# Second visit of a two-pass mixing: a switch from plain products to the seven-product scheme after block 5

## The chip, the cores and the metric

The kernel runs on one core of one Trainium2 chip. The metric is the device time of one execution in microseconds, as the median over the runs shown. Beside it there is one execution recorded by the hardware profiler. Names of engines: PE is TensorE (PEld its weight loads), DVE is VectorE, ACT is ScalarE, POOL is GpSimd and SP is SyncE.

## What is computed

The input is a batch of 8 sequences of 5696 positions with 128 channels. A long convolution by FFT comes first, and a mixing over positions follows. The reference, cut to what matters:

```python
# y: output of the convolution, (8, 5696, 128)
theta = y @ w_theta
zr, zi = y * cos(theta), y * sin(theta)
u = y + einsum('ts,bsd->btd', w_tok_r, zr) + einsum('ts,bsd->btd', w_tok_i, zi)
out = u + maximum(u @ w_ch, 0)
```

The change lies in the two einsums. Each is a 5696 x 5696 matrix, read in float32 and used in bfloat16, times a 5696 x 1024 operand.

## The kernel before

**Tiles and passes.** The 5632 positions that make up 44 whole tiles of 128 are cut into two halves of 22 tiles; a remainder of 64 is handled apart. The inner dimension is cut in two passes (p = 0 and 1), and in each pass it is cut into 11 blocks (j = 0 to 10). One *visit* (p, tt) makes four output banks of 128 x 512: two output tiles, tt and 22 + tt, for two halves of the batch. Pass 0 makes the visits tt = 0, 1, 2 and so on; "visit 1" below is its second one, tt = 1. Each visit walks through the 11 blocks in four *stretches* of 3, 3, 3 and 2 blocks. The program numbers the stretches through: visit 0 has stretches 0 to 3, visit 1 has 4 to 7, and visit 2 has 8 to 11.

**Two ways of doing one block.** The work of a visit is a 2 x 2 matrix of weights (w11, w12, w21, w22) times a 2 x 2 matrix of operands (b11, b12, b21, b22). A *plain* block takes 8 products of two matmuls each, 16 matmuls in all, straight into the four output banks. The *seven-product* scheme, in the order M3, M4, M5, M2, M1, M7, M6 (`ORDER`), takes 7 products of two matmuls each, so 14 per block. For these it needs sums of weights (`w_sum`, line 924, five for each stretch: M5, M2, M1, M7, M6) and sums of operands (`sum_ops`, line 852, five for each block, kept for all later visits of the pass). It accumulates in seven banks. At the end of the visit, 12 additions on DVE (line 1349) put the seven banks together into the four outputs. A plain visit of pass 0 instead adds its addend on PE (lines 1307 and 1310) and copies the four banks out on ACT (line 1312). `plain(p, tt)` (line 641) says that visits 0 and 1 of pass 0, and visit 0 of pass 1, are plain.

**Weights.** POOL issues the loads (line 690) into a ring of six slots (`ring`, `pump`); a slot comes free when the last stretch that reads it has been transposed. Four loads make a chunk: blocks 0 to 5 or blocks 6 to 10 of one visit. DVE transposes each stretch's four weights (`w_t`, line 915). `prepare(i)` writes these transposes and, for the seven-product scheme, the weight sums of stretch i. It is called at the head of stretch i - 1, so the program has them one stretch ahead. In the last stretch of a visit its steps are woven between the products instead.

**Buffers for the weight sums.** Transposed weights live in a pool of five buffers. Weight sums live in another, `sumpool`, with four (line 871), and a plain stretch also puts its w21 and w22 there.

**The operand sums of pass 0.** `owed` lists the five sums of each block. The first three write new tiles. The last two overwrite b12 and b21, which plain products still read. `sum_some(n)` (line 860) writes up to n of those that are allowed: sums 0 to 2 at any time, and sums 3 and 4 once `done["used"]` has passed the block. A plain stretch calls it up to nine times (six in the last one), and a seven-product stretch seven times.

**Order of the work.** From visit 0 to the middle of visit 2 (the end of stretch 9), `tc.manual_schedule(engines={DVE})` holds DVE to the order in which the program writes its instructions. Outside of it, and for the other engines, a planner orders instructions by the program's order and its own estimate of when they are ready.

**Background work.** `aside` puts a piece of other work into each stretch but the last of a visit. Its first half is four transposes on PE (line 943) and a copy on ACT (line 945). Its second half, `phases_b`, is four matmuls (line 574), then ACT, then DVE (line 578), then ACT (lines 598, 599, 602), then DVE (lines 612 and 613), then stores. It uses the tiles `red` and `mag`, or in the second stretch of a visit the buffers `c2` and `c3`.

Of the kernel before, what the change touches and what calls it, by code (L numbers as in the profile page):

```python
# [22 lines left out]
def kernel(  # L23
# [44 lines left out]
    NJ = QR // 64  # L68
    CJ = 6
    TJ = 3  # L70
# [564 lines left out]
    CHUNKS = [(j0, min(CJ, NJ - j0)) for j0 in range(0, NJ, CJ)]  # L635
# [2 lines left out]
    ring = {"n": 0, "read": set(), "wl": 0, "upto": 0}  # L638
    loaded = {}

    def plain(p, tt):

        return tt == 0 or (p == 0 and tt == 1)

    def loads_of(k):

        p, tt, c = chunks[k]
        loaded[k] = {}

        def one(n, a, row0, ng):  # L650
            loaded[k][n] = load_w(a, row0, p, *CHUNKS[c], ng=ng)
        if tt is None:
            return [lambda n=n, a=a: one(n, a, 2 * H, 2) for n, a in enumerate((moe_w_tok_r, moe_w_tok_i))]
        src = [(a, h * H + tt * P, 4) for h in range(2) for a in (moe_w_tok_r, moe_w_tok_i)]
        return [lambda n=n: one(n, *src[n]) for n in ((0, 1, 2, 3) if plain(p, tt) else (0, 3, 1, 2))]

    queue = [(k, f) for k in range(len(chunks)) for f in loads_of(k)]
    first_of = {}
# [160 lines left out]
    bts_of = {0: {}, 1: {}}  # L819
# [30 lines left out]
    def sum_ops(bt):  # L850
        b11, b12, b21, b22 = (bt[q] for q in (M2, M6, M7, M5))
        return [lambda f=f, x=x: f(*x) for f, x in (  # L852
            (nc.vector.tensor_sub, (bt[M3], b12, b22)), (nc.vector.tensor_sub, (bt[M4], b21, b11)),
            (nc.vector.tensor_add, (bt[M1], b11, b22)), (nc.vector.tensor_add, (b12, b11, b12)),
            (nc.vector.tensor_add, (b21, b21, b22)))]

    done = {"used": 0}
    owed = []

    def sum_some(n):  # L860

        for o in [o for o in owed if o[1] <= 2 or done["used"] > o[0]][:n]:
            owed.remove(o)
            o[2]()

# [25 lines left out]
        spread.extend(bg_phase(t, h) for t in list(range(24, 34)) + [22, 23, 44] + list(range(34, 44)) for h in range(2))  # L891
        spread.extend(bg_left(g) for g in range(0, NT, 4))

    for j in [*range(1, 6), 0, *range(6, NJ - 2), NJ - 1, NJ - 2]:
        owed += [(j, k, lambda j=j, k=k: sum_ops(bts_of[0][j])[k]()) for k in range(5)]

    def next_steps(n):
        for _ in range(min(n, len(steps1))):
# [114 lines left out]
    tags, where_bg = {"n": 0}, {}  # L1013
# [69 lines left out]
    for k, (p, tt, c) in enumerate(chunks):  # L1083
        j0, nj = CHUNKS[c]
        for s0 in range(0, nj, TJ):
            stretches.append((k, p, tt, j0, s0, min(TJ, nj - s0)))
    def prepare(i, at_once=True):
        if i >= len(stretches):
            return None
        k, p, tt, j0, s0, nj = stretches[i]  # L1090
        pump()

        def read():
            if s0 + nj == CHUNKS[chunks[k][2]][1]:
                ring["read"].add(k)
                pump()
        if tt is None:
            a1, a2 = (w_t(loaded[k][n], s0, nj, ng=2) for n in range(2))
            read()
            return a1, a2, w_sum(a1, a2, add, nj, m=64)  # L1100
        w11, w12, w21, w22 = (loaded[k][n] for n in range(4))
        if plain(p, tt):
            a = {}

            def some(n):
                if n in (0, 1):
                    a[n] = w_t((w11, w12)[n], s0, nj)
                elif n in (4, 5):
                    a[n - 2] = w_t((w21, w22)[n - 4], s0, nj, pool=sp)
            if not at_once and p:  # L1110
                return a, some
            for n in range(6):
                some(n)
                if p and n in (1, 4):
                    late_sums(8 if n == 1 else 4)
            read()
            return a if at_once else (a, lambda n: None)
        a = {}

        def step(n):  # L1120

            if n == 0:
                a[M3] = w_t(w11, s0, nj)
            elif n == 1:
                a[M4] = w_t(w22, s0, nj)
            elif n == 2:
                a["12"] = w_t(w12, s0, nj)
                a[M5] = w_sum(a[M3], a["12"], add, nj)
            elif n == 3:
                a["21"] = w_t(w21, s0, nj)  # L1130
                a[M2] = w_sum(a["21"], a[M4], add, nj)
            elif n == 4:
                a[M1] = w_sum(a[M3], a[M4], add, nj)
            elif n == 5:
                a[M7] = w_sum(a["12"], a[M4], ALU.subtract, nj)
            else:
                a[M6] = w_sum(a["21"], a[M3], ALU.subtract, nj)
        if at_once:
            for n in range(7):
                step(n)  # L1140
            read()
            return a
        return a, step
# [3 lines left out]
    for i, (k, p, tt, j0, s0, nj) in enumerate(stretches):  # L1147
# [4 lines left out]
        first_of_pair = j0 + s0 == 0  # L1152
        end_of_pair = j0 + s0 + nj == NJ
# [28 lines left out]
        def aside(first_of, second_of, *banks):  # L1182
            nonlocal second
            if first_of and spread and (p == 1 or (tt > 0 and not end_of_pair)):
                where_bg["tags"] = ("c2", "c3") if j0 + s0 == TJ else ("red", "mag")
                _, first, second = spread.pop(0)
                with tc.issue_after(sides["late"].ins) if p == 0 and tt == 1 else ExitStack():
                    first(*banks)
                    if len(spread) > 1:
                        spread[1][0]()  # L1190
            if second_of and second is not None:
                second()
                second = None

        if tt is None:
# [6 lines left out]
            for j in range(nj):  # L1202
                jj = j0 + s0 + j
                for r in range(2):
# [3 lines left out]
                    for k_ in range(2):  # L1208
                        for h, t in enumerate(terms):
                            nc.tensor.matmul(ps[64 * h:64 * h + 64], t[2 * k_][:, j, :64, r], b[t[2 * k_ + 1]],  # L1210
                                             start=st_ and k_ == 0, stop=sp_ and k_ == 1)
# [5 lines left out]
            if end_of_pair:  # L1217
# [5 lines left out]
                c, c0 = c_last  # L1223
                nc.vector.tensor_add(c, c0, ps)
                finish(p, NT - 1, 0, c)
            continue
        classic = plain(p, tt)
        if first_of_pair and i:
            ms = [mps.tile([P, 512], F32, tag=f"m{q}", name=f"m{q}") for q in (range(7) if not classic else (M3, M4, M5, M2) if p else (M2, M6, M1, M7))]
        if first_of_pair:  # L1230
            where = ((tt, 1), (22 + tt, 0), (tt, 0), (22 + tt, 1))
            if zl is not None:
                wl = [wl_room(), wlp.tile([P, P], BF16, tag="wl1", name="wl1")]
                for n in range(2):
                    nc.sync.dma_start(wl[n], wl_hbm[:, 22 * n + tt, :])
        if j0 + s0 == (3 if classic else 2) * TJ:
            cs = (sides["cs"] if p == 0 and tt == 0 else
                  [addend(p, n, t, h) for n, (t, h) in enumerate(where)])

# [33 lines left out]
        if i == 3:  # L1273
            (c12, z12), (c21, z21), (c11, z11), (c22, z22) = cs
            for h, out_of in enumerate((((c11, z11), (c21, z21)), ((c12, z12), (c22, z22)))):
# [5 lines left out]
                for n, (c, z) in enumerate(out_of):  # L1281
# [3 lines left out]
                    else:  # L1285
                        for b in range(4):
                            nc.tensor.matmul(m_[:, b * D:(b + 1) * D], z[:, b, :], ident_bf,
                                             start=False, stop=(b == 3))
                    nc.scalar.activation(c, m_, AF.Copy)
            done["used"] = 0  # L1290
        elif classic:
            for n in range(4):
                for j in range(nj):
                    product(a, j0 + s0 + j, j, n, range(2))
                    if p == 0 and (n * nj + j) % 4 != 3:
                        sum_some(1)
                if end_of_pair and n % 2:
                    (c12, z12), (c21, z21), (c11, z11), (c22, z22) = cs
                    out_of = (((c11, z11, 0), (c12, z12, 1)), ((c21, z21, 2), (c22, z22, 3)))[n // 2]
                    for h, (c, z, m_) in enumerate(out_of):  # L1300
                        if p:
                            nc.tensor.matmul(ms[m_], wl[n // 2], zl[h], start=False, stop=True)
                            nc.vector.tensor_tensor(c, z, ms[m_], op=add)  # L1303
                            late_sums(2 if n == 1 and h else 0)
                            continue
                        if n == 1:
                            nc.tensor.matmul(ms[m_], ident_bf, z, start=False, stop=True)
                        else:
                            for b in range(4):
                                nc.tensor.matmul(ms[m_][:, b * D:(b + 1) * D], z[:, b, :], ident_bf,  # L1310
                                                 start=False, stop=(b == 3))
                        nc.scalar.activation(c, ms[m_], AF.Copy)
                aside(n == 0, n == 2)
# [1 line left out]
                for n_ in range(7):  # L1315
                    step(n_)
            if p == 0:
                done["used"] = tt * (j0 + s0 + nj)
            else:
                late_sums(0 if end_of_pair else 3)  # L1320
                sums_1 += [op for j in range(nj) for op in sums_of(j0 + s0 + j, 3, 5)]
        else:
# [4 lines left out]
            if end_of_pair:  # L1327
# [3 lines left out]
                        M2: ((c21, c21, add), (c22, c22, ALU.subtract)),  # L1331
                        M1: ((c11, c11, add), (c22, c22, add)),
                        M7: ((c11, c11, add),), M6: ((c22, c22, add),)}
            for o in [o for o in owed if o[0] < j0 + s0 + nj]:
                owed.remove(o)
                o[2]()
            for n, q in enumerate(ORDER):
                sum_some(1)
                for j in range(nj):
                    jj = j0 + s0 + j  # L1340
                    for r in range(2):
                        nc.tensor.matmul(ms[q], a[q][:, j, :, r], bts[jj][q][:, r, :],  # L1342
                                         start=(jj == 0 and r == 0),
                                         stop=(jj == NJ - 1 and r == 1 and q not in left))
                if q in left:
                    nc.tensor.matmul(ms[q], left[q][0], left[q][1], start=False, stop=True)  # L1346
# [60 lines left out]
```

## Time and profile before

| | us |
|---|---|
| median of the three runs | 2030.79 |
| lowest and highest run | 2027.86, 2031.87 |
| the profiled execution, whole | 2025.06 |
| its span, from the first to the last instruction | 2023.3 |
| PE busy in the span | 1951.1 (96%) |
| DVE busy in the span | 1537.9 (76%) |

Mean granted clock of PE over the profiled execution is 0.989 of full speed. The span is what the rows of the profile cover, and all starting times in them count from its beginning. The profiled execution takes 1.76 us more than its span, and its 2025.06 us lie 5.73 us under the median of the runs.

In a timeline row, the first number is the start and the second the length from the start of the first to the modelled end of the last instruction merged into the row. Brackets hold the idle time of the engine before the row and what ended it. Matmul ends are modelled and overlap the next start, so the step from one start to the next is the cost of a matmul in a stream.

### The profile page before, as it was taken

Reading aid. Unit: us, or ns where it says so; the run is one execution under the profiler, and the core shown is the slowest. Engines: PE = TensorE matmul, PEld = TensorE weight load, DVE = VectorE, ACT = ScalarE, POOL = GpSimd, SP = SyncE. Lnnn points to the kernel's source line nnn. Section 1 sums busy time; section 2 is a strip of 40 time slices with the busy share of each in tenths; the row PEclk is TensorE's granted clock in tenths of the full one; section 3 lists DMA queues with packets and bytes.
Section 4 is the critical chain, followed back from the end, with each engine's and each line's share of the span. In section 5 each row is a group of like instructions: output and inputs, shape, how many; then the busy total and the mean of one; then the engine's idle time right before and its main releaser. Section 6 shows DMA issues by size and latency. Waiting matters only on the chain.

```text
span 2023.3 us, 42629 instructions
## 1 busy us (share of the span) xinstructions
PE 1951.1 (96%) x16289; PEld 1075.2 (53%) x16289; DVE 1537.9 (76%) x2822; ACT 636.0 (31%) x934; POOL 984.7 (49%) x1799
## 2 busy tenths in 40 slices
PE   7799898889999999999999999999999999999998
PEld 5689898644444444444444444444444444444444
DVE  8788787666778787878777768777677776867767
ACT  7688787853233323332200000011111111111111
POOL 9434313574454545364666454544535445354550
PEclk9899899999999999999999999999999999999999
DMA  9999988999898989899999699887978879687783
GB/s 118 193 174 155 152 177 217 259 239 190 143 182 172 183 166 165 178 173 179 168 167 157 123 256 227 127 150 128 153 128 150 145 133 153 126 154 138 138 153 86
DMA packets 506222, 332.49 MB, mean 164 GB/s; under 512 B 186471, under 2 KB 458663, under 8 KB 505927
## 3 DMA queue, kind: packets, MB, share of 16 engines
q0 software_dynamic: 323616, 160.42, 61.5%
q1 hardware_dynamic: 174528, 156.22, 25.9%
q10 hardware_dynamic: 7872, 13.11, 1.9%
q8 instruction: 128, 2.10, 0.4%
q14 instruction: 78, 0.64, 0.1%
HBM read 373.24 MB, written 92.95 MB: 230 GB/s over the span
## 4 chain that ended last, share of the span: by engine, by line
PE 64%; DMA 4%; DVE 3%; issue 1%; POOL 1%; ACT 0%; DVEq 0%; ACTq 0%; SPq 0%; POOLq 0%
PE m L1342 60%; DMA ring<-in_moe_w_tok_i_dram 3%; DVE c L1349 1%; PE v L1002 1%; PE utp L995 1%; POOL ring L690 1%; PE m L1346 1%; DMA ring<-in_moe_w_tok_r_dram 1%; DVE wt L915 1%; PE theta_ps L574 0%; DVE b L852 0%; PE tpz L943 0%; DMA out_dram<-c 0%; DMA yT<-yt_hbm 0%; DMA wl<-in_moe_w_tok_i_dram 0%
## 5 line engine op out<-in xcount | busy, mean ns | idle before, releaser
L690 POOL DMA_DIRECT2D ring<-in_moe_w_tok_i_dram x720 | 388.9, 546 | 666.4 <-DVE wt L915 572.0
L690 POOL DMA_DIRECT2D ring<-in_moe_w_tok_r_dram x720 | 387.2, 546 | 120.6 <-DVE wt L915 72.3
L915 DVE STREAM_TRANSPOSE wt<-ring 128x384 f32<-128x384 f32 (+2 forms) x720 | 359.5, 524 | 113.1 <-PE m L1342 78.3
L1342 PE MATMUL m<-b,wt 128*128 128x512 bf16 x1640 | 388.3, 379 | 1.9 <-DVE wt L915 1.7
L1342 PEld LDWEIGHTS <-wt 128*128 128x128 bf16 x1804 | 176.0, 98 | 215.5 <-DVE wt L915 4.3
L1349 DVE TENSOR_TENSOR c<-c,m 128x512 f32<-128x512 f32 x412 | 266.2, 671 | 0.4 <-DMA out_dram<-c 0.4
L997 ACT ACTIVATE ring<-utp 128x512 bf16<-128x512 bf16 x85 | 50.7, 597 | 571.9 <-PE utp L995 571.9
L460 PE MATMUL ps<-r_u,uv_t 128*128 128x128 f16 x1024 | 117.1, 220 | 5.6 <-DVE g__8853 L467 1.8
L992 ACT ACTIVATE ub<-c 128x512 bf16<-128x512 f32 x88 | 55.2, 628 | 197.6 <-DVE c L1303 116.8
L1243 PE MATMUL m<-b,wt 128*128 128x512 bf16 x480 | 112.9, 383 | 4.1 <-DMA b<-zz 3.3
L461 PE MATMUL ps<-r_v,uv_t 128*128 128x100 f16 x1024 | 114.9, 208 | 0.1
L153 POOL DMA_DIRECT2D x<-in_x_dram x128 | 97.9, 770 | 19.4 <-POOL x L151 14.1
L461 PEld LDWEIGHTS <-uv_t 128*128 128x128 f16 x1024 | 100.5, 98 | 6.4 <-issue 5.2
L440 DVE TENSOR_TENSOR uv_t<-xs,hs 128x2048 f16<-128x2048 f16 x77 | 91.4, 1223 | 14.1 <-ACT xs L438 9.2
L460 PEld LDWEIGHTS <-uv_t 128*128 128x128 f16 x1024 | 100.6, 98 | 2.1 <-DVE uv_t L445 1.7
L438 ACT ACTIVATE xs<-ps 128x1024 f16<-128x1024 f32 x96 | 90.7, 973 | 35.0 <-PE ps L271 13.1
L1243 PEld LDWEIGHTS <-wt 128*128 128x128 bf16 x528 | 50.7, 99 | 61.7 <-issue 7.7
L576 ACT ACTIVATE red<-theta_ps,magic 128x512 f32<-128x512 f32 (+1 forms) x46 | 31.6, 687 | 153.3 <-PE theta_ps L574 89.4
L271 PEld LDWEIGHTS <-w_t 64*128 64x128 f16 x3240 | 57.3, 99 | 29.7 <-issue 23.3
L945 ACT ACTIVATE ring<-tpz 128x512 bf16<-128x512 bf16 (+1 forms) x46 | 27.5, 597 | 137.0 <-PE tpz L943 123.2
L251 PE MATMUL ps<-f_t,x 89*128 89x180 f16 x512 | 61.8, 249 | 2.6 <-DVE a__240 L366 0.9
L1004 DVE SCALAR_TENSOR_TENSOR c<-v,c 128x512 f32<-128x512 f32 x88 | 60.1, 684 | 3.2 <-PE v L1002 2.1
(2935 smaller groups left out, 3766.0 us busy)
## 6 DMA issues: line engine op xcount, KB each, us to landing
ring<-in_moe_w_tok_r_dram POOLq DMA_DIRECT2D x352, 96.0 KB, 4.4
ring<-in_moe_w_tok_i_dram POOLq DMA_DIRECT2D x352, 96.0 KB, 4.8
ring<-in_moe_w_tok_r_dram POOLq DMA_DIRECT2D x352, 80.0 KB, 4.4
ring<-in_moe_w_tok_i_dram POOLq DMA_DIRECT2D x352, 80.0 KB, 3.7
cp_hbm<-c SPq DMA_DIRECT2D x88, 256.0 KB, 2.4
c<-cp_hbm SPq DMA_DIRECT2D x88, 256.0 KB, 3.8
out_dram<-c SPq DMA_DIRECT2D x88, 256.0 KB, 4.2
hs<-hf_hbm SPq DMA_DIRECT2D x77, 256.0 KB, 3.5
```

The lines of the kernel that those rows point to most:

```text
L153: nc.gpsimd.dma_start(x16[p0:p1, e, n0:n0 + 16, :HD], bass.AP(tensor=src.tensor, offset=src.offset + (p0 * N2 + n0) * D + dh * HD, ap=[[N2 ...
L251: nc.tensor.matmul(ps[:, i // 2, (i % 2) * 2 * K1:(i % 2 + 1) * 2 * K1], lhs(q + i), f1_t[:NB], start=True, stop=True)
L438: nc.scalar.activation(xs[:, :, :, :ck], ps, AF.Copy)
L440: nc.vector.tensor_tensor(uv[:, :, :, c0:c0 + ck], xs.rearrange("p e d k -> p e (d k)").unsqueeze(1).to_broadcast([P, 2, 2, HD * CK]), hv. ...
L460: nc.tensor.matmul(o, u_t[:, at:at + P], r_u, start=True, stop=False)
L461: nc.tensor.matmul(o[:, 2 * NP:], v_t[:, at:at + P], r_v, start=False, stop=True)
L690: nc.gpsimd.dma_start(wb[32 * i:32 * i + 32, :ng, :nj * 64], bass.AP(tensor=a.tensor, offset=a.offset + row0 * S + p * H + i * QR + j0 * 6 ...
L915: nc.vector.transpose(wt.rearrange("p j t r -> p (j t r)").bitcast(F32).rearrange("p (j g t) -> p g j t", j=TJ, g=4)[:, :ng, :nj], wb[:, : ...
L1004: nc.vector.scalar_tensor_tensor(c[:m], v[:m], 0.0, c[:m], op0=ALU.max, op1=ALU.add)
L1243: nc.tensor.matmul(ms[n // 2 * 2 + h], a[n][:, j, :, r], bts_of[p][jj][n % 2 * 2 + h][:, r, :], start=(n % 2 == 0 and jj == 0 and r == 0), ...
L1342: nc.tensor.matmul(ms[q], a[q][:, j, :, r], bts[jj][q][:, r, :], start=(jj == 0 and r == 0), stop=(jj == NJ - 1 and r == 1 and q not in left))
L1349: nc.vector.tensor_tensor(c, z, ms[q], op=op)
```

## The change

Visit 1 of pass 0 is split. Blocks 0 to 5 (stretches 4 and 5) stay plain. At the end of stretch 5 the addends are added on PE, and ACT copies the four banks into the four `c` tiles. Blocks 6 to 10 (stretches 6 and 7) go by the seven-product scheme into seven newly taken banks. At the end of stretch 7, the 12 additions on DVE add these banks to the `c` tiles.

For this the operand sums of blocks 6 to 10 have to be ready before stretch 6. `done["raw"]` allows their last two sums as soon as visit 0 is done. The list `owed` is put in another order: first the sums 0 to 2 of all blocks, then sums 3 and 4 of blocks 6 to 10, then sums 3 and 4 of blocks 0 to 5. The loads of visit 1's second chunk come in the order of the seven-product scheme. The addends are fetched in stretch 5, and the background work of that stretch uses `red` and `mag`, since `c2` and `c3` are taken.

```diff
-    def plain(p, tt):
+    def plain(p, tt, j):
-        return tt == 0 or (p == 0 and tt == 1)
+        return tt == 0 or ((p, tt) == (0, 1) and j < CJ)
...
-        for o in [o for o in owed if o[1] <= 2 or done["used"] > o[0]][:n]:
+        for o in [o for o in owed if o[1] <= 2 or done["used"] > o[0] or CJ <= o[0] < done["raw"]][:n]:
...
-    for j in [*range(1, 6), 0, *range(6, NJ - 2), NJ - 1, NJ - 2]:
-        owed += [(j, k, lambda j=j, k=k: sum_ops(bts_of[0][j])[k]()) for k in range(5)]
+    landed = [*range(1, CJ), 0, *range(CJ, NJ - 2), NJ - 1, NJ - 2]
+    for js, ks in ((landed, range(3)), (landed[CJ:] + [*range(CJ)], range(3, 5))):
+        owed += [(j, k, lambda j=j, k=k: sum_ops(bts_of[0][j])[k]()) for j in js for k in ks]
...
-                where_bg["tags"] = ("c2", "c3") if j0 + s0 == TJ else ("red", "mag")
+                where_bg["tags"] = ("c2", "c3") if j0 + s0 == TJ and not mixed else ("red", "mag")
...
-        classic = plain(p, tt)
-        if first_of_pair and i:
+        classic = plain(p, tt, j0)
+        mixed = (p, tt) == (0, 1)
+        change = mixed and j0 + s0 == CJ
+        if (first_of_pair or change) and i:
...
-        if j0 + s0 == (3 if classic else 2) * TJ:
+        if j0 + s0 == (1 if mixed else 3 if classic else 2) * TJ:
...
-            done["used"] = 0
+            done["raw"] = NJ
...
-                if end_of_pair and n % 2:
+                if (end_of_pair or mixed and j0 + s0 + nj == CJ) and n % 2:
...
-                done["used"] = tt * (j0 + s0 + nj)
+                done["used"] = j0 + s0 + nj
+                if j0 + s0 + nj == CJ:
+                    cs = [(c, c) for c, _ in cs]
...
-            for o in [o for o in owed if o[0] < j0 + s0 + nj]:
+            for o in [o for o in owed if j0 + s0 <= o[0] < j0 + s0 + nj]:
...
-                                         start=(jj == 0 and r == 0),
+                                         start=(jj == (CJ if mixed else 0) and r == 0),
```

## The prediction

> **What bounds the kernel now.** I read the table of busy time by stretch of time first, cut at the edges of the visits, then DVE's timeline over visits 1 and 2, then PE's waits, then the granted clock around PE's idle times.
>
> ```profile
> core 0: us, PE busy (x) PEld busy (x) DVE busy (x) ACT busy (x) POOL busy (x), PEclk, DMA share, GB/s
> 461.00:501.00 40.00, 40.00 (x207) 18.97 (x206) 28.77 (x54) 13.38 (x22) 18.84 (x36) 1.00 1.00 185
> 501.00:538.00 37.00, 34.92 (x185) 16.45 (x184) 23.65 (x50) 12.30 (x20) 17.17 (x32) 1.00 0.83 146
> 575.00:611.00 36.00, 36.00 (x186) 17.09 (x185) 29.42 (x61) 11.21 (x18) 17.16 (x32) 1.00 0.94 183
> ```
>
> Visit 1 (461 to 501), visit 2 (501 to 538) and a later one: PE is busy throughout, but for 2.1 us in visit 2. From 545 us to the end, PE's waits add up to only 5 us (the largest row is 1.7). So a delay of PE here is carried to the end of the kernel, and so is a gain. DVE in visit 1 has 40 - 28.8 = 11.2 us idle. The question is whether that idle time can be used.
>
> ```profile
> 468.64 1.95 DVE L915 STREAM_TRANSPOSE wt<-ring 128x384 f32<-128x384 f32 x4
> 470.87 0.69 DVE L578 SCALAR_TENSOR_TENSOR red<-red,mag 128x512 f32<-128x512 f32 x1 [0.28 <-ACT mag L577]
> 473.01 0.43 DVE L612 TENSOR_TENSOR red<-red,ring 128x512 bf16<-128x512 f16 x1 [1.45 <-ACT red L599]
> 473.62 0.42 DVE L613 TENSOR_TENSOR mag<-mag,ring 128x512 bf16<-128x512 f16 x1 [0.18 <-ACT mag L602]
> 473.97 1.49 DVE L915 STREAM_TRANSPOSE wt<-ring 128x384 f32<-128x384 f32 x3
> ...
> 484.86 1.42 DVE L915 STREAM_TRANSPOSE wt<-ring 128x256 f32<-128x256 f32 x4
> 486.20 3.66 DVE L852 TENSOR_TENSOR b<-b 128x1024 bf16<-128x1024 bf16 x6
> ...
> 515.27 0.56 DVE L924 TENSOR_TENSOR out__11354<-wt 128x768 bf16<-128x768 bf16 x1 [3.55 <-PE m L1342]
> 515.74 2.49 DVE L852 TENSOR_TENSOR b<-b 128x1024 bf16<-128x1024 bf16 x4
> 518.15 0.68 DVE L578 SCALAR_TENSOR_TENSOR red<-red,mag 128x512 f32<-128x512 f32 x1
> ...
> 521.24 1.49 DVE L915 STREAM_TRANSPOSE wt<-ring 128x384 f32<-128x384 f32 x3
> ...
> 539.36 1.25 DVE L1349 TENSOR_TENSOR c<-c,m 128x512 f32<-128x512 f32 x2
> ```
>
> The row at 515.27 tells most. It is the weight sum M6 of stretch 9, the fifth sum in a pool of four buffers, so it waits until PE has used M5 of the same stretch. The four operand sums, the background step (L578 to L613) and the transposes of stretch 10 stand behind it in the written order; DVE did none of them during those 3.55 us. PE then ran out of work:
>
> ```profile
> PE m L1342 <- DVE wt L915: 1.5, 1, 1.5
> ```
>
> That is stretch 10, started at 521.87 instead of about 520.4. This pattern, four sums behind a blocked M6, is what the change brings into visit 1 with more in it.
>
> **Durations.** From rows above and their neighbours: a full transpose 0.49 us (1.95 / 4), a short one (two blocks) 0.36; an operand sum 0.617 (3.70 / 6 at 495.58); a weight sum 0.50 full, 0.41 short; an addition L1349 0.645 (1.28 / 2 in the four double rows at 570.67 to 573.39); a background step 3.2 (L578 at 470.87 to the next transpose, 1.45 of it waiting for ACT); a 128x512 matmul 0.2165 (24 in 5.18 at 547.30).
>
> **What the change removes and adds.** PE: five blocks of 14 instead of 16 matmuls, 10 x 0.2165 = -2.2 us. The addends (2 x 0.43 us) and ACT's four copies (1.08 a pair) only move to the end of stretch 5; the first banks that they hold up, M1 and M7, are wanted 5 us later. The order of two weight loads, the earlier fetch of addends on SP and seven banks instead of four cost nothing I can see: the addends' buffers are free and nothing waits for them. DVE: ten weight sums (5 x 0.50 + 5 x 0.41 = 4.6), twelve additions (7.7), and the four operand sums that stood in visit 2 (2.5): 14.8 us more in visit 1, against 11.2 idle; and 9, 7 and 6 operand sums now stand in stretches 4, 5 and 6, where there were 0, 6, 6 and 6 in 4 to 7.
>
> **DVE's order, step by step.** The same reckoning on the order of before, from 461.0 and 468.64 on, gives 521.8 for stretch 10 with a wait of 1.47; the trace has 521.87 and 1.46. For the order after:
> - Stretch 4: DVE is free at 470.6. Seven sums (to 474.9), background step (478.1), two sums: 479.4. Before, it had begun stretch 6's transposes at 474.0.
> - Stretch 5: four transposes and three weight sums take it to 482.9. M7 waits 0.4 for a buffer of the plain stretch. M6 is the fifth sum: it waits for PE's M5 of stretch 6. PE ends stretch 5 with its addends at 483.5, then M3, M4, four transposes and M5 take it to 487.6. So DVE stands 4.0 us until 487.8. Behind it: M6 itself, seven operand sums (492.65), background step (495.9), then the first short transpose of stretch 7: 496.2.
> - PE ends stretch 6 at 483.5 + 42 x 0.2165 + 0.43 = 493.0 and waits for that transpose: **3.2 us**.
> - Stretch 7's weights (to 499.4), five operand sums (502.5), background step (505.7), one sum (506.4); then, as written, four additions for M3 and M4 (508.9) and the first transpose of stretch 8: 509.4. PE ends stretch 7 at 496.2 + 28 x 0.2165 = 502.3 and waits **7.1 us**.
> - In stretch 8, M2 and M1 each wait for DVE, which has two additions, a transpose and a weight sum per product against 1.3 us of PE: 0.9 + 0.5 = **1.4 us**. PE ends it at 520.4.
> - Stretch 9: no operand sums are left, so after M6 and a background step the transposes of stretch 10 are ready at 528.9, and PE, done at 529.9, doesn't wait: the old 1.5 us are gone.
>
> Sum at the start of stretch 10: 3.2 + 7.1 + 1.4 - 2.2 - 1.5 = +8.0 (529.9 against 521.87).
>
> **Clock.** PE idle for 2.53 us before 446.56 was followed by a granted clock of 0.62 over 4.5 us; idle for 1.46 before 521.87 was not:
>
> ```profile
> 446.50:451.00 4.50, 4.39 (x12) 1.56 (x13) 4.50 (x9) 0.00 (x0) 3.93 (x8) 0.62 0.79 241
> 521.80:526.00 4.20, 4.13 (x26) 2.13 (x27) 3.99 (x10) 1.38 (x3) 1.50 (x3) 1.00 0.58 128
> ```
>
> A mean of 0.62 is half speed for 2 x 0.38 x 4.5 = 3.4 us, so 1.7 us lost. Behind the 3.2 us wait this would be hidden, since stretch 7 may end up to 3 us later before it delays an addition. Behind the 7.1 us wait it comes on stretch 8, where 1.4 us of waits for DVE absorb it. Bounds: 0 to 2 us; I take 0.4, near the low end, because of that cover. The Trainium skill, page "TensorE: Matmul & The Clock Gate", section "Part 1: The HAM clock gate", has the clock halved after an idle window of about 3.4 us: by that rule the first wait would cost no clock at all; the row with 2.53 us says that it can. The sum is the same by either, since that loss is hidden.
>
> **What follows in visit 2.** Four waits of PE between 530 and 545 (0.4, 0.2, 0.6, 0.7: 1.9 in all) are of the same kind. DVE enters stretch 10 1 us ahead instead of 1.5 late, which speaks for fewer; weights loaded 12 us later than before (stretch 7's transposes free their slots at 496 to 498 instead of 485 to 486) speak for more. Bounds -1.9 to +1.9; I take 0, halfway, as the rows speak for both.
>
> **Sum.** +8.0 + 0.4 + 0 = +8.4 us: 2025.06 becomes 2033.5 for the profiled execution, and on the median, 5.73 above it, 2039.2, say 2039. With the bounds, +6.1 to +11.9: 2036.9 to 2042.7.
>
> **Rivals.**
> - *DVE is not held to the written order, or the idle time is used* (16%): faster. Over visits 1 and 2 together DVE has 77 - 52.4 = 24.6 us idle and gets 14.8 - 2.5 = 12.3 more, so the work would fit. PE gains 2.2 and the old 1.5, up to 1.9 with the later waits: -3.7 to -5.6, so 2025 to 2027 on the median. It decides if DVE runs the ready operand sums while M6 waits. The 3.55 us at 515.27 speak against it; most of this chance is for an order in stretches 6 and 7 that I read wrongly.
> - *M6 of stretch 6 finds a buffer* (8%): the 4.0 us wait falls away, all behind it comes 4 us earlier or is bound by the additions alone; the same reckoning gives 525.3 for stretch 10, +3.6, so 2034.4. The four plain-visit buffers would have to come free sooner; the waits at 505.75 and 515.27 speak against it.
> - *The weights come late too* (5%): slots freed 12 us late let DVE wait for a load in stretches 9 to 11, as it did for 2.23 us at 477.69 when DMA was full (share 1.00 in visit 1, 0.83 in visit 2): +8.4 + 2 to 4, so 2041 to 2043.
> - *The split doesn't take hold* (2%): no change, 2030.8.
>
> **How the numbers follow.** The forecast keeps 69%. Measurements of this kernel can tell about 0.2% (4.1 us) from no change. Slower by more: forecast, late weights and half of the second rival with its error, 77%. Faster by more: most of the first rival, 13%. Within: 10%. The range leaves out the first rival, takes in the second's lower edge and the bounds of the forecast, with 1 to 2 us at the upper end for runs that differ by 4 (2027.86 to 2031.87): 2031 to 2044.
>
> **What would show it.** In the changed kernel's DVE timeline: a weight sum with a wait of about 4 us for PE near 488, seven L852 behind it, and L1349 rows only from about 506. In PE's waits: about 3 us and 7 us for L915 near 496 and 509, and none near 530. ACT's copies L1312 near 478 and 484. DVE's idle time in visit 1 should shrink to the M6 wait and the waits inside background steps. I am wrong if PE runs through 493 to 510 without a wait above 2 us, if operand sums run while M6 waits, or if the delay at stretch 10 is made up before 600 us.

## The result, and the profile after

The median went from 2030.79 to 2039.74 us (11 runs of each). The ratio is 1.0042, with a 95% interval of 1.0029 to 1.0056, so 8.5 us slower, between 5.9 and 11.4 (the medians themselves lie 8.95 us apart). The forecast was 2039, for 8.4 us. The profiled execution took 2042.28 us, with a span of 2040.5.

The two profiled executions lie 17.2 us apart, nearly twice the difference of the medians, so they have to be cut before they are compared. The order of the instructions up to visit 1 is the same in both kernels, yet PE's first product of visit 1 started at 461.24 in the trace of before and at 466.05 in that of after. These 4.8 us come ahead of anything that the change touches. From that product on, the comparison is clean, and this document uses one measure for all traces: the time from PE's first product of visit 1 to its first product of stretch 10. It is 60.63 us before and **71.62 us** after. At the start of visit 8 the distance is 10.5 us. The remaining 1.9 us came up far behind the change, between visit 18 and the end, most of it in the first visit of the second pass. There PE waits 2.2 us for the landing of operands (`b<-z_hbm`) in the trace of after; in a second trace of the same kernel it waits 2.8 us for transposes and loses 2.7 us, and the trace of before has neither wait. Of the ten traces below with all or part of the change, seven lose from 0.9 to 2.7 us there; the other three, and the three controls without it, gain from 0.1 to 0.8. Whether the change has a part in this is not shown.

The table of busy time of the changed kernel, cut where its stretches begin: stretches 4 and 5 in the first row, then 6, 7 with the wait behind it, 8, and 9. Columns as in the table of before: length, busy time (and instructions) of PE, PEld, DVE, ACT and POOL, granted clock, DMA share, GB/s.

```profile
466.00:488.50 22.50, 22.34 (x123) 10.95 (x124) 17.52 (x32) 6.75 (x12) 10.06 (x19) 1.00 1.09 207
488.50:501.10 12.60, 9.44 (x49) 4.25 (x47) 8.31 (x17) 4.06 (x8) 0.00 (x0) 0.99 0.12 33
501.10:516.60 15.50, 8.78 (x41) 4.26 (x43) 11.84 (x25) 5.42 (x9) 8.58 (x16) 0.83 0.96 161
516.60:527.90 11.30, 11.28 (x44) 4.78 (x44) 10.88 (x22) 0.00 (x0) 2.58 (x5) 0.80 0.37 108
527.90:537.60 9.70, 9.33 (x46) 4.33 (x46) 4.66 (x10) 3.37 (x6) 5.97 (x12) 1.00 1.07 150
```

PE, which had no idle time in visit 1 before, is idle for 3.2 us in stretch 6 and the wait behind it, and for 6.7 us in stretch 7 and the wait behind it. Stretch 8 is nearly without idle time and takes 11.3 us at a granted clock of 0.80; at full clock its busy time would be about 9 us. DVE's timeline over the same time (start, length, instruction, count, idle time before it and what ended it):

```profile
479.51 0.68 DVE L578 SCALAR_TENSOR_TENSOR red<-red,mag 128x512 f32<-128x512 f32 x1
483.91 0.43 DVE L612 TENSOR_TENSOR red<-red,ring 128x512 bf16<-128x512 f16 x1 [3.72 <-ACT red L599]
...
489.69 0.55 DVE L925 TENSOR_TENSOR out__11079<-wt 128x768 bf16<-128x768 bf16 x1
492.85 0.56 DVE L925 TENSOR_TENSOR out__11081<-wt 128x768 bf16<-128x768 bf16 x1 [2.61 <-PE m L1347]
493.33 0.68 DVE L852 TENSOR_TENSOR b<-b 128x1024 bf16<-128x1024 bf16 x1
493.93 1.28 DVE L852 TENSOR_TENSOR ring<-ring 128x1024 bf16<-128x1024 bf16 x2
495.13 2.49 DVE L852 TENSOR_TENSOR b<-b 128x1024 bf16<-128x1024 bf16 x4
497.54 0.68 DVE L578 SCALAR_TENSOR_TENSOR red<-red,mag 128x512 f32<-128x512 f32 x1
...
500.62 1.09 DVE L916 STREAM_TRANSPOSE wt<-ring 128x256 f32<-128x256 f32 x3
...
505.61 0.43 DVE L925 TENSOR_TENSOR out__11208<-wt 128x512 bf16<-128x512 bf16 x1 [1.46 <-PE m L1347]
...
512.65 2.47 DVE L1354 TENSOR_TENSOR c<-c,m 128x512 f32<-128x512 f32 x4
515.05 1.03 DVE L916 STREAM_TRANSPOSE wt<-ring 128x384 f32<-128x384 f32 x2
```

The row at 492.85 is the fifth weight sum, M6 of stretch 6. It started 0.2 us after PE had begun the product behind M5, as forecast, and the seven operand sums and the background step stand behind it. The transposes of stretch 7 start at 500.62, and PE's first product of stretch 7 at 501.12. The additions L1354 start at 512.65, and the transposes of stretch 8 follow them at 515.05. PE's waits from 440 to 570 us (what waited, for what, us in total, times, longest):

```profile
PE theta_ps L574 <- ACT ring L946: 4.3, 3, 3.6
...
PE m L1347 <- DVE wt L916: 3.1, 1, 3.1
PE tpz L944 <- ACT mag L577: 2.9, 1, 2.9
```

The middle row is the wait before stretch 7. The wait before stretch 8 appears under two other names. The planner had put background matmuls of stretches 8 and 9 into this gap (L574 at 512.87, L944 at 516.13). These were waiting too, for ACT, which waited for DVE's background step and its stores. PE's last product of stretch 7 ended at 509.03 and the next started at 516.62, so the gap is 7.6 us, with about 1 us of short background matmuls in it. The transpose of stretch 8's first weights ended at about 515.6, so DVE was ready 1 us before the gap ended. The last 1 us belongs to L944.

### The profile page after: what moved, and what is told of

The parts are those of the page before. It is cut to its first block, busy times and chain, and to the rows that moved or that the text cites. A ratio compares the mean times of both kernels' runs of the same rounds, so it can differ in the third digit from the quotient of the medians.

```text
span 2040.5 us, 42459 instructions
## 1 busy us (share of the span) xinstructions
PE 1948.1 (95%) x16103; PEld 1079.3 (53%) x16279; DVE 1548.0 (76%) x2844; ACT 635.9 (31%) x934; POOL 983.9 (48%) x1799
## 4 chain that ended last, share of the span: by engine, by line
PE 40%; DMA 4%; DVE 2%; POOL 2%; issue 2%; ACT 0%; DVEq 0%; POOLq 0%; ACTq 0%
PE m L1347 37%; DMA ring<-in_moe_w_tok_i_dram 3%; POOL ring L690 2%; DVE c L1354 1%; PE v L1003 1%; PE utp L996 1%; PE m L1351 1%; DMA ring<-in_moe_w_tok_r_dram 1%; DVE wt L916 0%; DMA wl<-in_moe_w_tok_r_dram 0%; PE m L1211 0%; DVE b L852 0%; DMA wl<-in_moe_w_tok_i_dram 0%; POOL wl L963 0%; DVE c L1005 0%
## 5 line engine op out<-in xcount | busy, mean ns | idle before, releaser
L916 DVE STREAM_TRANSPOSE wt<-ring 128x384 f32<-128x384 f32 (+2 forms) x720 | 358.9, 522 | 116.8 <-PE m L1347 74.1
L1347 PE MATMUL m<-b,wt 128*128 128x512 bf16 x1619 | 391.8, 381 | 5.7 <-DVE wt L916 3.4
L1347 PEld LDWEIGHTS <-wt 128*128 128x128 bf16 x1824 | 178.7, 98 | 224.1 <-DVE wt L916 8.6
L1354 DVE TENSOR_TENSOR c<-c,m 128x512 f32<-128x512 f32 x424 | 272.8, 668 | 0.4 <-PE m L1347 0.4
L440 DVE TENSOR_TENSOR uv_t<-xs,hs 128x2048 f16<-128x2048 f16 x77 | 91.3, 1221 | 14.2 <-ACT xs L438 10.4
L1246 PE MATMUL m<-b,wt 128*128 128x512 bf16 x392 | 93.9, 383 | 7.3 <-DMA b<-zz 3.3
L1246 PEld LDWEIGHTS <-wt 128*128 128x128 bf16 x448 | 42.9, 99 | 55.1 <-issue 9.5
```

Of the source, the lines that this page charges most:

```text
L440: nc.vector.tensor_tensor(uv[:, :, :, c0:c0 + ck], xs.rearrange("p e d k -> p e (d k)").unsqueeze(1).to_broadcast([P, 2, 2, HD * CK]), hv. ...
L916: nc.vector.transpose(wt.rearrange("p j t r -> p (j t r)").bitcast(F32).rearrange("p (j g t) -> p g j t", j=TJ, g=4)[:, :ng, :nj], wb[:, : ...
L1246: nc.tensor.matmul(ms[n // 2 * 2 + h], a[n][:, j, :, r], bts_of[p][jj][n % 2 * 2 + h][:, r, :], start=(n % 2 == 0 and jj == 0 and r == 0), ...
L1354: nc.vector.tensor_tensor(c, z, ms[q], op=op)
```

## The experiments

The measure, in us, with the reckoning's value where one was made ahead of the run. "Visit 8" is the distance from the kernel before at the start of visit 8, and the last column the ratio of the run times to those of the kernel before, run beside it, with its 95% interval.

| kernel | reckoned | measured | visit 8 | ratio |
|---|---|---|---|---|
| before | 60.6 | 60.63 | 0 | 1 |
| changed kernel, two traces | 68.7 | 71.62, 72.00 | +10.5, +11.2 | 1.0042 (1.0029 to 1.0056), 1.0044 (1.0027 to 1.0061) |
| M6 late | 63.8 | 67.13 | +6.5 | 1.0033 (1.0022 to 1.0045) |
| M6 late, copies late | 64.8 to 65.4 | 66.32 | +5.2 | 1.0020 (1.0005 to 1.0035) |
| no additions | 64.7 | 69.12 | +8.1 | 1.0043 (1.0027 to 1.0059) |
| no background in visit 1 | 60.7 | 61.39 | -0.3 | 1.0006 (0.9994 to 1.0019) |
| DVE's order free | 58.3 | 60.18 | -3.2 | 0.9985 (0.9967 to 1.0002) |
| held, order written anew | 57.2 to 59 | 58.84 | -4.6 | 0.9977 (0.9960 to 0.9995) |
| free, no background, two traces | 56.4, 55.7 | 55.73, 55.73 | -7.7, -7.7 | 0.9960 (0.9941 to 0.9978), 0.9966 (0.9948 to 0.9985) |
| before, order free | 59.1 | 59.23 | -4.2 | 0.9989 (0.9973 to 1.0005) |
| before, no background | 59.3 | 59.29 | -1.5 | 0.9994 (0.9977 to 1.0011) |
| before, free, no background | 57.9 | 57.89 | -5.5 | 0.9972 (0.9954 to 0.9990) |

The expectations reckon with durations a little shorter than the prediction's: for the changed kernel they give 68.2 instead of the 68.7 that follows from the prediction (529.9 - 461.24). Where background work is taken out of visit 1 it is done in later visits, so that part of what is saved at stretch 10 is given back there: the control "before, no background" gains 1.3 us in the measure.

**M6 late.**

```diff
-            for n in range(7):
+            split = (p, tt) in ((0, 1),)
+            for n in range(6 if split else 7):
...
+            if split:
+                late_m6[i] = lambda: step(6)
...
+        if i + 1 in late_m6:
+            late_m6.pop(i + 1)()
```

> The changed kernel, with one thing moved: the weight sum M6 of stretches 6 and 7 is written after the operand sums and the background step of the stretch before, instead of ahead of them. Measure: the time from PE's first matmul of visit 1 to its first matmul of stretch 10 (before 60.6 us, changed kernel 71.6 us; the reckoning alone, without the clock, gave 68.2 for the latter). Theory (DVE held to the written order, with M6 blocked for lack of a buffer, makes PE wait): DVE no longer stands still before M6 of stretch 6; PE's 3.1 us wait before stretch 7 goes, a wait of 2 to 5.5 us before stretch 8 stays because the work itself is too much. By the reckoning 63.8 us, so 4.4 us less than the changed kernel by it and 4 to 8 less than its trace. Rival A (the buffers are not the point, DVE simply has too much work): the order of work on DVE changes nothing in the sum, so 71 +- 1 us. Rival B (PE is held by the background work's place in its own queue and by the clock): PE still waits about 3.5 and 3 us at the background matmuls, so 69 to 71 us.

Measured: 67.13 us, 4.5 less than the changed kernel, so the blocked M6 and what stands behind it is a real part of the loss. PE's 3.1 us wait before stretch 7 is gone. In its place PE waits 1.4 us inside stretch 6 for M6 itself (the row of L1352 below), so 1.5 of the 4.5 us are gained ahead of stretch 7 and the rest behind it. And 3.3 us more are left than reckoned. PE's waits in this kernel:

```profile
PE theta_ps L574 <- ACT ring L946: 3.8, 3, 3.1
...
PE tpz L944 <- ACT mag L577: 2.5, 1, 2.5
PE m L1352 <- DVE out__11190 L925: 1.4, 1, 1.4
```

Two causes show in its trace. DVE was later with stretch 7's transposes than reckoned: they began at 492.80, 31.9 us into the measure, where the prediction's own steps, put in this order, give about 30.6 (482.9, 0.4 of waiting, M7, seven sums, the background step, M6, less 461.24). And the first product of stretch 8 started at 508.04, 1.9 us after its weights had been transposed, since L944 stood ahead of it in PE's queue and waited for ACT's L577. Neither rival's forecast (71, and 69 to 71) fits, but what B points at adds 1.9 us to the theory.

**Copies late.** The next kernel tests the first of the two causes. In the changed kernel, ACT's queue is:

```profile
480.23 0.63 ACT L598 ACTIVATE mag<-red 128x512 f32<-128x512 f32 x1 [4.59 <-DVE red L578]
482.68 0.60 ACT L1315 ACTIVATE c<-m 128x512 f32<-128x512 f32 x1 [1.81 <-PE m L1310]
483.17 0.71 ACT L599 ACTIVATE red<-red,zero_b 128x512 f16<-128x512 f32 x1
```

The copy L1315 of the first two banks stands between L598 and L599 of a background step and waits 1.81 us for PE's addends. DVE's L612 waits for L599: 3.72 us at 483.91 above, where the kernel before has 1.45 in each of its three such rows of visit 1.

```diff
-                if (end_of_pair or mixed and j0 + s0 + nj == CJ) and n % 2:
+                if (end_of_pair and n % 2) or (mixed and j0 + s0 + nj == CJ and n == 3):
...
+                    out_of = out_of[0] + out_of[1] if mixed else out_of[n // 2]
```

> The changed kernel with M6 of stretches 6 and 7 late, and in addition all four addends and ACT's four copies at the very end of stretch 5 instead of two after half of it. Same measure (67.1 us with M6 late alone). Theory: the first pair of copies stands in ACT's queue ahead of L599 of stretch 4's background step and waits there 2.2 us for PE; DVE's L612 then waits 4.1 us instead of 1.45. With the copies late this wait is 1.45 again, all of DVE's work behind it comes 1.7 to 2.6 us earlier, and stretch 10 with it: 64.8 to 65.4 us. Rival (ACT's order is off the path): 67 us, no change.

Measured: 66.32 us, 0.8 less. Stretch 7 began 1.55 us earlier than with M6 late alone (32.00 against 33.55 us into the measure) and stretch 8 2.1 us earlier (45.01 against 47.13), which is the forecast effect. Stretch 8 itself then took 11.55 instead of 10.24 us and gave 1.3 of it back, at a granted clock of 0.78 against 0.88. So ACT's copies do lengthen DVE's work, by 1.6 us at stretch 7 and 2.1 at stretch 8; in the changed kernel this is hidden by M6's wait, which shrank from the reckoned 4.0 to 2.6 us.

**No additions.**

```diff
-                    for c, z, op in (sums[q][::-1] if i + 1 == len(stretches) and q == M5 else sums[q]):
+                    for c, z, op in () if mixed else (sums[q][::-1] if i + 1 == len(stretches) and q == M5 else sums[q]):
```

> The changed kernel without the twelve additions on DVE at the end of visit 1 (left out: the seven-product half of that visit does not reach the output). Same measure. Theory: the wait before stretch 7 stays at 3.1 us; the wait before stretch 8 falls by the four additions ahead of its first transpose, 2.4 us, and the two waits inside stretch 8 go. By the reckoning 64.7 us, 3.5 us less than with the additions. Rival C (the additions are the whole cost): the wait before stretch 8 goes, about 60 us. Rival B (background work in PE's queue): hardly any change, 70 us or more.

Measured: 69.12 us. The wait before stretch 7 is again 3.1 us, and stretch 8 begins 2.7 us earlier than in the changed kernel, near the 2.4 of the four additions ahead of its transpose. But it still takes 11.29 us, as with the additions. DVE's row for the fifth weight sum waits 3.1 us for PE there, so inside stretch 8 DVE is ahead; what makes it long is the granted clock, 0.50 over its first 4.1 us. The additions are worth 2.5 us, not 3.5, and by no means the whole loss. Rival C (about 60 us) and rival B (70 or more) do not fit. The ratio of run times is too coarse to show this difference.

**No background work in visit 1.**

```diff
-            if first_of and spread and (p == 1 or (tt > 0 and not end_of_pair)):
+            if first_of and spread and (p == 1 or (tt > 1 and not end_of_pair)):
```

> The changed kernel, with the background work of visit 1 (stretches 4, 5, 6) moved to later visits; nothing is left out. Same measure (before 60.6, changed 71.6 us). Theory: three background steps of 3.2 us less on DVE's written order, M6 of stretch 6 still blocked for about 4 us. By the reckoning 60.7 us: no wait before stretch 7, about 3.6 us before stretch 8 and 1.1 inside it. PE's waits at the background matmuls (L574, L944) in visit 1 go too. Over the whole kernel 1.3 us of PE's background work come back later, so about +1 us against before and -8 against the changed kernel. Rival A (total DVE work): the same direction, but the M6 block would not be seen and PE would not wait at all, 57 to 58 us. Rival C (the additions at the end of visit 1 alone make the wait before stretch 8): that wait stays at about 7 us, so 65 us or more.

Measured: 61.39 us. No wait before stretch 7, and a gap of 3.6 us between stretches 7 and 8 (reckoned 3.6). M6 of stretch 6 is still blocked, for 3.77 us:

```profile
488.04 0.56 DVE L925 TENSOR_TENSOR out__11053<-wt 128x768 bf16<-128x768 bf16 x1 [3.77 <-PE m L1347]
```

So the blocked M6 alone does not make PE wait; it takes the background steps in DVE's queue as well. The loss against the kernel before is gone to within the run times (1.0006, 0.9994 to 1.0019). The control is the same move in the kernel before:

> Control: the kernel before, DVE held as written, with only the background work of visit 1 moved to later visits. Measure: PE's first matmul of visit 1 to its first of stretch 10 (before 60.6 us). Theory: PE saves its 1.3 us of background matmuls in visit 1, keeps the 1.5 us wait before stretch 10, and pays the 1.3 us later: 59.3 us, and within 1 us of before for the whole kernel. The 8 to 10 us that the same move saved in the changed kernel (61.4 against 71.6) would then be DVE time that only the changed kernel lacks. If instead the kernel before also gains several us, the background work is what costs, with or without the change.

Measured: 59.29 us, 1.3 less than before, which is PE's own time for the background matmuls. The same move saved 10.2 us in the changed kernel, so about 9 of them are waits that the changed kernel alone has, with DVE's queue full. Against this control the kernel with the change still loses 2.1 us (61.39 against 59.29): in the written order, less work alone does not make the change pay.

**DVE's order free.**

```diff
-        elif (p, tt, j0 + s0) in ((0, 2, 6), (1, 1, 0)):
+        elif (p, tt, j0 + s0) in ((0, 1, 0), (1, 1, 0)):
             ordered.close()
```

> The changed kernel with the hold on DVE's written order ended at the start of visit 1 (stretch 4) instead of in visit 2; from there the planner orders DVE. Nothing is left out. Same measure. Theory (the written order, not the amount of DVE work, makes the loss): the planner puts operand sums, transposes and additions into the waits of the background steps, and both long waits of PE go; only about 1.2 us inside stretch 8 stay. Reckoned along the planned order with the same durations: 58.3 us, 2.3 less than before, so the whole kernel 1 to 3 us faster than before. Rival A (DVE has too much work for visit 1 in any order): at least 4 us of PE waits stay before stretch 8, 63 us or more.

Measured: 60.18 us. The busy times over the whole measure (same columns as above):

```profile
466.52:526.70 60.18, 57.36 (x298) 27.13 (x302) 52.73 (x103) 20.17 (x34) 28.64 (x54) 1.00 0.87 166
```

DVE does the same work, 52.7 us of it (53.3 in the changed kernel), and PE is idle for 2.8 us (60.18 - 57.36) instead of 10.4. Rival A falls: the order, not the amount of work, made most of the loss. Most of what is left goes back to one row of DVE's timeline:

```profile
500.96 0.69 DVE L578 SCALAR_TENSOR_TENSOR red<-red,mag 128x512 f32<-128x512 f32 x1 [4.04 <-ACT mag L577]
```

This background step could start only when ACT had written `mag`, and ACT waited for the stores of the step before it; all three steps of visit 1 use `red` and `mag` now. Other tiles for the second step were not tried. The control, the same edit in the kernel before:

> The kernel before, with the hold on DVE's written order ended at the start of visit 1, as in the changed kernel with the free order. Nothing is left out. Measure: PE's first matmul of visit 1 to its first of stretch 10 (before 60.6 us; changed kernel with free order 60.2). Theory: only the 1.5 us wait before stretch 10 goes, as there is nothing else to win, so 59.1 us and 0 to 2 us for the whole kernel. If the free order by itself makes the kernel faster by more than the change with it does (2.3 us less from visit 1 to the end in its trace), the seven-product half is worth nothing even with a free order; if it gives less, the ten matmuls are worth the difference.

Measured: 59.23 us, less than the 60.18 with the seven-product half. So with the background work in place the seven-product half is worth nothing even in a free order; it loses 0.9 us. What makes the free order look good is the old wait before stretch 10 and the ones behind it: both kernels gain another 2.8 us between stretch 10 and visit 8 (table).

**Held, order written anew.** The same hold as before and after, but M6 late in visits 1 and 2, no background work in visit 1, and the sums of blocks 3 to 5 allowed from stretch 8 on:

```diff
+            split = (p, tt) in ((0, 1), (0, 2))
+            for n in range(6 if split else 7):
...
+        if (p, tt, j0 + s0) == (0, 2, 0):
+            done["used"] = NJ
...
-                done["used"] = j0 + s0 + nj
+                done["used"] = min(j0 + s0 + nj, TJ)
```

> The changed kernel, DVE held to the written order as before, but with the order written anew: M6 after the operand sums in visits 1 and 2, no background work in visit 1 (done in later visits), the sums of blocks 3 to 5 in stretch 8. Nothing is left out. Same measure. Theory: with the blocked M6 out of the way and 3 x 3.2 + 3.7 us less on DVE in visit 1, PE waits about 1.1 us in stretch 8 and not before stretches 7, 8 and 10. By the reckoning 57.2 us, up to 59 if background matmuls of stretch 8, put ahead of its first product, hold PE as they did for 1.3 us in the kernel without background work; for the whole kernel 1 to 3 us less than before, as 1.3 us of background matmuls come back later. Rival A (too much DVE work in any order): above 61 us.

Measured: 58.84 us and 0.9977. A held order can carry the change without a loss; 1.7 us of waiting for ACT at one background matmul and 0.8 for a weight sum are left. What the seven-product half is worth in this order is not known, since the kernel before was not run with it.

**Free order and no background work.** Both edits in the changed kernel:

> The changed kernel with both edits: DVE's order left to the planner from visit 1 on, and no background work in visit 1 (moved to later visits; nothing is left out). Same measure. Theory: the 1.8 and 0.7 us waits that are left with the free order come from a background step that waits for its tiles' stores (DVE 4.0 us at L578); without it PE hardly waits: 60.2 - 2.5 - 1.3 = 56.4 us, and 2 to 4 us less than before for the whole kernel. Rival A (DVE's work is the bound): waits of PE before or in stretch 8 stay at 2 us or more, 58.5 us or more.

Its control, both edits in the kernel before:

> Control: the kernel before with both edits of the fastest kernel so far (DVE's order free from visit 1, background work of visit 1 moved), but with visit 1 plain throughout. Same measure (the fastest one, with the seven-product half: 55.7 us). Theory: visit 1 without any wait costs ten matmuls more, 2.2 us, so 57.9 us at stretch 10; for the whole kernel 2 us slower than the fastest one, 1 to 3 us faster than before. Rival: the seven-product half is worth nothing once the order is free, 55 to 56 us.

And the two kernels that are compared most, once more, beside the control:

> The fastest kernel so far again (seven-product half, free order, no background work in visit 1), beside its control on the same chip. Theory: 55.7 us at stretch 10 again, 2 us less than the control, and 0.2 to 0.5% less than before for the whole kernel.

> The changed kernel again, for a second trace on the same chip as the others. Theory: the waits from visit 1 to stretch 10 repeat (71.6 us, to within the 1 to 2 us that the clock after a wait can differ); the 4.8 us by which visit 1 started later than in the trace of before do not belong to the change and can come out at any value from -3 to +6.

Measured: 55.73 us, twice, against 57.89 for the control. The difference is 2.16 us, and ten matmuls by 0.216 are 2.16.

```profile
458.85:514.58 55.73, 55.73 (x280) 26.00 (x277) 48.83 (x94) 9.20 (x16) 29.23 (x55) 1.00 0.87 154
```

PE is busy from end to end at full clock. This is the one setting tried in which the change gives what it removes, and it beats both given kernels: 0.9960 and 0.9966 of before, where the control has 0.9972. The intervals overlap, so the 2.16 us are shown by the traces, at stretch 10 and at visit 8, and not by the run times. Nor are they there at the end of the traces: counted from visit 1, the two kernels with the change end 5.0 and 4.3 us ahead of before and the control 5.1, since the former lose 2.1 and 2.7 us between visit 18 and the end, where the control gains 0.2. The cause of that is open, as said above. The changed kernel repeated its 71.62 with 72.00 us, and its visit 1 began at 462.18, so the 4.8 us ahead of visit 1 did not repeat.

## Why the prediction was right

**The bound.** PE's waits did set the time: the distance at stretch 10 (11.0 us) was 10.5 at the start of visit 8 and was not made up by the end.

**The first wait** (forecast 3.2 us, for the transposes of stretch 7): 3.1 in both traces, at 501.12, which is 35.07 us into the measure against 35.0 reckoned. That M6 with the queue behind it was the cause is shown from two sides: with M6 late the wait is gone, and without the background steps it is gone although M6 stays blocked. The way there differs in one step. That the addends and ACT's four copies "only move to the end of stretch 5" was wrong: a copy in ACT's queue held a background step for 2.3 us more. M6's wait took it up.

**The second wait** (forecast 7.1 us): the gap is 7.6 us. It did not appear under the name L915 (L916 in the changed kernel), because the planner filled it with background matmuls; who looks only for the forecast row would have called it wrong.

**The waits inside stretch 8** (forecast 1.4 us): they don't show as waits. The clock took their place, as the cover for the clock term said: stretch 8 took 11.3 us, against 11.0 reckoned with the waits.

**The old 1.5 us wait before stretch 10** is gone, and the three named waits behind it (0.4, 0.6 and 0.7) are the same as before to 0.1 us; taking 0 for visit 2 was right.

**The clock term was too small**, the term of the sum that was mis-sized. 0.4 us was taken, with 2 as the upper bound. The measured 71.62 exceeds the reckoning's 68.7 by 3.0 us. Of these 1.3 came because half speed in stretch 7 made M6 of stretch 7 wait 1.46 us for PE (row at 505.61), with all of DVE's queue behind it; this is read from the trace and was not tried by itself. Another 1.0 came from the background matmul L944 ahead of stretch 8, which the working did not have, and the kernel with M6 late shows this wait too (1.9 us). Stretches 8 and 9 took 0.3 us each more than reckoned: stretch 8 at a granted clock of 0.80, stretch 9 at 1.00 but with a wait of 0.32 us of a background matmul for ACT. What failed is "Behind the 3.2 us wait this would be hidden": it looked at the additions and not at the blocked M6 ahead of them. A wait of 3.1 us was followed by half speed, as the row with 2.53 us had said it can be, and it cost time. The Trainium skill, page "TensorE: Matmul & The Clock Gate", section "Part 1: The HAM clock gate", has an idle window of about 3.4 us for that; the waits of 3.1 us in both traces were shorter.

**The match of the number is in part luck.** The working gave 8.4 us for stretch 10, where the two traces have 11.0 and 11.4; the median came out within 1 us of the forecast all the same. That the run times put the change at 8.5 and not at 11 us has no shown cause. Both traced executions of the changed kernel were above the median of their runs, by 2.5 us (2042.28 against 2039.74) and 2.9 us (2039.90 against 2037.02), but no trace shows where the faster ones saved it.

**Rivals.** "DVE is not held to the written order": DVE kept to it, since none of the seven sums behind M6 started while M6 waited. The free order shows that the idle time is there to be used once the order allows it. "M6 of stretch 6 finds a buffer" was priced at +3.6 us (525.3 less 521.87 is 3.4); it was not tried. M6 late, which clears the queue another way, gave +6.5, with 1.4 us of waiting for the late M6, the copies and the background matmul in it. "The weights come late too": no new wait for a weight load shows in the changed kernel between visit 1 and stretch 10. In the durations, 24 matmuls in 5.18 us are 0.216 each, not 0.2165; that moves no term by more than 0.03 us.

## What to carry to other kernels

In an engine that is held to a written order, one blocked instruction makes everything written behind it late: before adding work to such a queue, walk through it in order and mark where it stands still, since the idle time in a busy table is not free to use. Ten matmuls less on the bounding engine were worth exactly their 2.2 us in the visits around them, but only once the order was free and other work of the second engine had left the visit; at the end of the kernel the gain did not show. Cut two traces at the first instruction that the change touches, and measure from there.

## What the runs showed of the hardware

PE's clock in the changed kernel, in windows behind the first wait, inside the gap and behind it (columns as in the first table; the last three are granted clock, DMA share and GB/s):

```profile
501.10:504.50 3.40, 3.38 (x12) 1.52 (x13) 2.49 (x7) 0.97 (x2) 3.14 (x6) 0.55 0.75 130
504.50:509.00 4.50, 4.50 (x24) 2.09 (x23) 3.39 (x7) 0.60 (x1) 3.31 (x8) 1.00 1.25 203
514.00:516.60 2.60, 0.27 (x1) 0.21 (x2) 2.60 (x6) 1.28 (x2) 0.00 (x0) 0.57 0.63 146
516.60:521.50 4.90, 4.88 (x13) 1.83 (x13) 4.69 (x10) 0.00 (x0) 0.00 (x0) 0.53 0.29 108
521.50:527.90 6.40, 6.40 (x32) 2.95 (x31) 6.19 (x13) 0.00 (x0) 2.58 (x5) 1.00 0.43 108
```

A wait of 3.1 us was followed by half the granted clock for about 3.4 us, in both traces of the changed kernel: 2 x 0.45 x 3.4 = 3.1 us behind the wait, and 0.4 in its last 1.1 us, where the clock was 0.83. Behind a gap of 7.6 us with only 1 us of short matmuls in it the clock was half from inside the gap on, for 6.8 us (2 x 0.43 x 2.6 and 2 x 0.47 x 4.9), of which 4.6 us slowed products. In the second trace the windows from 505 to 512 and 512 to 519 have 0.69 and 0.58, so 10.2 us, longer still behind the same gap, and about 5 us of it slowed products. These three durations, 3.4, 6.8 and 10.2 us, are one, two and three times 3.4. A wait of 1.8 us in the kernel with the free order was followed by no drop (1.00 over its 60.18 us). And the traces of the nine kernels that hold DVE's order, with the same instructions ahead of visit 1, began that visit between 460.9 and 466.6 us, a spread of more than half of the effect that was to be measured.
